# Retention, a dense MoE and a routed MoE on one core: stores, block sums, pass changes and gate sweeps put in another order

## Chip, cores and metric

One core of a Trainium2 chip runs the whole program in one launch. The metric is device microseconds of an execution, taken as the median over runs.

## What is computed

The reference, cut to what matters: a retention (a linear attention with a decaying lower-triangular mask), then a mixture of four experts weighted by given probabilities, then a mixture of eight experts in which each row goes to exactly one expert of limited capacity.

```python
ret = (scale * q @ k.T) * Dmat            # 4 batches, 8 heads, 576 positions, 64 columns a head
x = (ret @ v) as (2304, 512)
p = domain_probs / (domain_probs.sum(-1) + 1e-9)
x = sum_e p[:, e] * (relu(x @ w1[e]) @ w2[e])                     # 4 experts, 512 -> 1024 -> 512
logits = x @ w_gate                                               # 8 experts
rows go to experts greedily by falling logit, at most 288 each
out[row] = relu(x[row] @ moe2_w1[e]) @ moe2_w2[e]
```

All data are 32-bit. The matmuls of both MoE split each operand into a high and a low part (a rounded copy, and the rest) and add three products.

## The kernel before

**Retention** (lines 462 to 623) takes 16 pairs of heads, each as a chain of nine chunks of 64 positions. A chunk is a few 64x64 matmuls (L522, L524), a copy of the state on ScalarE (L533), a masked copy of the scores on VectorE (L535) and the output matmuls (L546); the next chunk of the same pair waits for the copies. Several pairs run interleaved. `finish` multiplies the outputs by the decay (L562 into the tiles `xr` of the first pass, L567 into `xf` tiles) and stores the `xf` tiles to the DRAM tensor `xs` (L573) for the later passes. The order is written by a list scheduler, `Graph`: each operation has an engine, a cost and a bias, and at each step the ready operation of the highest priority goes next. Where the plan leaves TensorE too thinly used, the scheduler sets in small bf16 matmuls (`filler`, L593), a fixed number of them. The same graph carries the preparation of the first MoE: block sums of x (`x_add`, L358, tables `SUMS`), their splits into high and low (`x_split`, L362 and L363, seven tiles x0 to x6; `LOW` names the engine of each low part), and the first two weight blocks `w1_ops(0)` and `w1_ops(1)` (L398 to L400), with their loads (L377) and stores (L384, L385) on the queue of SyncE (SP).

**The first MoE** (lines 626 to 955) makes three passes of 768 rows; a pass has 16 steps `k` (four experts by four blocks of weights), 48 in all. One step uses seven block products (Strassen-like: `step(k, "a")` to `step(k, "g")`, 42 matmuls of 384 columns at L666), each of which needs one x tile and one of the weight parts wa, wt, wb. Between the products stand up to three second-layer tiles of 12 matmuls (`y_next`, L716). Product f of a step goes on in the PSUM bank P, from which `keep(k, 3)` copies on ScalarE (L673) after product e; product g goes on in R, which VectorE reads (`add`, L677) after that copy. So f waits for ScalarE and g for VectorE. The other operations of a step are written by hand between these calls: `some(n)` emits n operations of the weight block of the next step (`early`), `w2_split` splits a second-layer weight (L653, L654), `spare` gives one turn to a side job, `halves` (L448, L449) in the first two passes and `late` in the third. ScalarE, VectorE and GpSimd (POOL) work off their queues in the order written.

At a **pass change** (`turn_`, k = 15 and 31) the seven x tiles are rebuilt from four tiles loaded from `xs`: sums (L358) after product c, then the splits (L362, L363) spread over c to g. All ten (or six) operations of the next weight block come at once after c (`full`); so it is at k = 1 also.

**The third pass's sweeps** (`late`, lines 764 to 810): for the gate logits of the middle rows VectorE makes 48 dot products of a row tile with a gate column (L796), and POOL makes 64 products of a weight tile with a gate column (L802), whose sums ScalarE takes (L791). They come in four sweeps over two gate columns each; in a sweep each turn of `spare` (nine a step) emits one dot product, as long as there are any, and two of three turns a POOL product.

After it the second MoE (from line 959) routes and runs the eight experts; the change doesn't touch its code.

## Time and profile before

| what | value |
|---|---|
| median of 3 runs | 1206.41 us |
| lowest and highest run | 1192.81 and 1209.75 us |
| the profiled execution's own time | 1208.07 us |
| its span, first to last instruction | 1206.3 us |
| mean granted TensorE clock of the span | 0.970 |
| retention, up to the first matmul of the first MoE (L666) | 0 to 127.7 us |
| first pass change, second pass change | near 365 and 626 us |
| third pass, to about | 900 us |

How to read the profile: times are microseconds from the span's start. PE is TensorE, PEld its weight loads, DVE VectorE, ACT ScalarE, SP the queue of SyncE. A row of the stretches gives each engine's busy time in a stretch, then the TensorE clock that was granted (1.00 is 2.4 GHz, 0.50 is 1.2 GHz; a value between is a stretch with both). A row of the timeline gives start, duration, engine, line, operation, and in brackets how long the engine stood idle before it and what ended that.

### The profile page before, as it was taken

Reading aid. Unit: us, or ns where it says so; the run is one execution under the profiler, and the core shown is the slowest. Engines: PE = TensorE matmul, PEld = TensorE weight load, DVE = VectorE, ACT = ScalarE, POOL = GpSimd, SP = SyncE. Lnnn points to the kernel's source line nnn. Section 1 sums busy time; section 2 is a strip of 40 time slices with the busy share of each in tenths; the row PEclk is TensorE's granted clock in tenths of the full one; section 3 lists DMA queues with packets and bytes.
Section 4 is the critical chain, followed back from the end, with each engine's and each line's share of the span. In section 5 each row is a group of like instructions: output and inputs, shape, how many; then the busy total and the mean of one; then the engine's idle time right before and its main releaser. Section 6 shows DMA issues by size and latency. Waiting matters only on the chain. (4 is left out here: it accounts for less than half of the span.)

```text
span 1206.3 us, 22262 instructions
## 1 busy us (share of the span) xinstructions
PE 1165.4 (97%) x8032; PEld 1016.4 (84%) x8032; DVE 716.6 (59%) x1628; ACT 558.0 (46%) x1262; POOL 622.3 (52%) x559
## 2 busy tenths in 40 slices
PE   9999899999999999999999898998999999999997
PEld 7777799999998999998889787887997887888876
DVE  4684466766667354454465767759346766666421
ACT  3442355555555555555453455554640233333332
POOL 5451167777764666766444878879530022222221
PEclk9995799999999999999999899999999999999999
DMA  9673388999984988889644544545311878887780
GB/s 338 199 263 97 113 287 306 331 322 319 334 280 146 314 272 298 300 289 318 224 123 161 195 145 156 198 144 173 99 58 60 322 315 319 319 318 307 301 340 29
DMA packets 125263, 284.43 MB, mean 236 GB/s; under 512 B 14048, under 2 KB 22624, under 8 KB 121056
## 3 DMA queue, kind: packets, MB, share of 16 engines
q1 hardware_dynamic: 121792, 273.23, 64.5%
q0 software_dynamic: 3216, 9.67, 2.2%
q8 instruction: 63, 1.03, 0.4%
q14 instruction: 48, 0.39, 0.1%
q10 hardware_dynamic: 144, 0.11, 0.0%
HBM read 209.00 MB, written 74.19 MB: 235 GB/s over the span
## 5 line engine op out<-in xcount | busy, mean ns | idle before, releaser
L716 PE MATMUL py<-w2h,h 128*128 128x512 f32 x1056 | 350.1, 392 | 0.5 <-ACT h L683 0.5
L716 PEld LDWEIGHTS py<-w2h,h 128*128 128x128 f32 x1056 | 198.3, 188 | 39.0 <-ACT h L683 1.6
L449 POOL TENSOR_TENSOR pair<-pv,pair 128x512 fp32r<-128x512 f32 x128 | 174.8, 1368 | 94.5 <-ACT pair L448 90.5
L716 PE MATMUL py<-w2l,h 128*128 128x512 f32 x528 | 205.5, 389 | 0.0
L673 ACT ACTIVATE sum<-P 128x384 f32<-128x384 f32 x144 | 70.2, 488 | 155.2 <-PE P L666 155.0
L400 POOL TENSOR_TENSOR wal<-r,wah 128x512 fp32r<-128x512 f32 x48 | 64.2, 1337 | 127.1 <-ACT wah L399 94.1
L654 POOL TENSOR_TENSOR w2l<-r,w2h 128x512 fp32r<-128x512 f32 x64 | 89.9, 1406 | 63.1 <-ACT w2h L653 63.0
L723 DVE SCALAR_TENSOR_TENSOR acc<-py,pr,acc 128x512 f32<-128x512 f32 x115 | 85.9, 747 | 56.8 <-PE py L716 56.2
L716 PEld LDWEIGHTS py<-w2l,h 128*128 128x128 f32 x528 | 99.3, 188 | 15.4
L802 POOL TENSOR_TENSOR pp<-pw,wgb 128x512 f32<-128x512 f32 x64 | 98.3, 1551 | 4.2 <-ACT pp L791 2.5
L400 DVE TENSOR_TENSOR wtl<-tw,wth 128x768 fp32r<-128x768 f32 x48 | 61.6, 1284 | 64.2 <-ACT wth L399 64.2
L448 ACT ACTIVATE pair<-pv 128x512 fp32r<-128x512 f32 x128 | 80.2, 627 | 33.9 <-DMA pv<-in_w1b 16.2
L684 DVE SCALAR_TENSOR_TENSOR h<-Q,h 128x384 fp32r<-128x384 f32 x96 | 53.5, 557 | 51.6 <-ACT h L683 51.6
L400 POOL TENSOR_TENSOR wbl<-r,wbh 128x512 fp32r<-128x512 f32 x48 | 77.5, 1615 | 12.7 <-ACT wbh L399 12.7
L229 PE MATMUL ph<-gh,ub 128*128 128x288 f32 x512 | 83.6, 300 | 0.5 <-DVE gl L256 0.3
L683 ACT ACTIVATE h<-Q 128x384 fp32r<-128x384 f32 x96 | 46.8, 487 | 69.8 <-DVE Q L677 69.3
L653 ACT ACTIVATE w2h<-r 128x512 fp32r<-128x512 f32 x96 | 60.3, 628 | 30.5 <-DMA r<-in_w2a 30.4
L229 PEld LDWEIGHTS ph<-gh,ub 128*128 128x128 f32 x512 | 72.3, 188 | 1.5 <-DVE gl L256 1.0
L522 PE MATMUL s<-X,Y 64*64 64x64 f32 x576 | 65.4, 246 | 4.4 <-DVE X L535 3.0
L533 ACT ACTIVATE Y<-s 64x128 f32<-64x128 f32 x128 | 33.7, 269 | 74.5 <-PE s L524 70.5
L1223 POOL DMA_INDIRECT xg<-x_rows,idx x14 | 16.0, 1139 | 99.4 <-DVE idx L256 83.0
L796 DVE SCALAR_TENSOR_TENSOR xt<-row,wgb 128x512 f32<-128x512 f32 x48 | 62.1, 1293 | 8.0 <-DMA row<-x_rows 7.9
(272 smaller groups left out, 2715.2 us busy)
## 6 DMA issues: line engine op xcount, KB each, us to landing
w_halves<-pair SPq DMA_DIRECT2D x64, 512.0 KB, 5.1
ub<-w_halves SPq DMA_DIRECT2D x32, 1024.0 KB, 8.7
r<-in_w2a SPq DMA_DIRECT2D x96, 256.0 KB, 5.2
r<-in_w1a SPq DMA_DIRECT2D x64, 256.0 KB, 4.2
pv<-in_w1b SPq DMA_DIRECT2D x64, 256.0 KB, 4.9
pv<-in_w2b SPq DMA_DIRECT2D x64, 256.0 KB, 5.5
w_low<-pair SPq DMA_DIRECT2D x64, 256.0 KB, 4.3
raw<-in_w2b SPq DMA_DIRECT2D x32, 512.0 KB, 6.6
```

The source lines that it names most:

```text
L229: self.add("pe", cost, lambda: self.nc.tensor.matmul(out, w, x, start=start, stop=stop, **kw), (w, x), (out,), chain=chain, cols=self.size(x))
L400: low = lambda e, i, x: lambda: e.tensor_tensor(w(i, 1), x(), r32(w(i, 0)), op=OP.subtract)
L448: nc.scalar.activation(pair[:, 0], r, AF.Copy)
L449: nc.gpsimd.tensor_tensor(pair[:, 1], r, r32(pair[:, 0]), op=OP.subtract)
L522: nc.tensor.matmul(score()[:, h], Y[lo, h, ch(c + 1)], X[lo, h, ch(c + 1)], start=True, stop=True)
L653: nc.scalar.activation(h, r, AF.Copy)
L654: (nc.vector if i and q < 2 * NPAIR // NP1 else nc.gpsimd).tensor_tensor(lo, r, r32(h), op=OP.subtract)
L673: nc.scalar.activation(sums[n], PS[k]["P"][:, :TG], AF.Copy)
L716: mm(y, x, w, start=(start and n == 0), stop=(stop and n == len(todo) - 1), **kw)
L723: nc.vector.scalar_tensor_tensor(x, y, s, x, op0=OP.mult, op1=OP.add)
L796: nc.vector.scalar_tensor_tensor(scr, row[t], 1.0, wgb[:, e - e0], op0=OP.mult, op1=OP.mult, accum_out=L[:, JT + t, e:e + 1])
L802: nc.gpsimd.tensor_tensor(pp, w[f], wgb[:, e - e0], op=OP.mult)
```

## The change

Two groups of edits. **Retention:** stores of `xf` are held, in the order of the SP queue, behind the load of the pair seven further on (`loads`, `stores`), for which there are four `xf` tiles a kind instead of two; the block sums and splits of x have a bias of 250 instead of 550 and higher planned costs; the first weight block keeps its place, and everything of the second (`w1_load(1)`, `w1_ops(1)`, its store) and the loads behind it come after the last pair's load and with no bias. **First MoE:** at the pass changes the sums have tiles of their own, are emitted after d instead of c, and the splits stand in another order, x1's low part on POOL (`TURN_LOW`); `full` is left to the steps `lone` (0 and 46), so at k = 1, 15 and 31 the next weight block is emitted 3, 3, 2 and 2 at a time, as in other steps; the sweeps run on without a stop between them, with single gate columns loaded ahead (`gate`, four buffers), a dot product at most every second turn and never of a later sweep than the POOL products. Two unused tables of the routing constants go.

```diff
-X_FIRST = 550.0
+X_FIRST = 250.0
...
-            return ("v", 0.86, lambda: nc.vector.tensor_tensor(raw[o], raw[x], raw[y], op=op), (f"r{x}", f"r{y}"), (f"r{o}",))
+            return ("v", 1.4, lambda: nc.vector.tensor_tensor(raw[o], raw[x], raw[y], op=op), (f"r{x}", f"r{y}"), (f"r{o}",))
...
-            en, cost = {"v": (nc.vector, 0.86), "pool": (nc.gpsimd, 1.75)}[e]
+            en, cost = {"v": (nc.vector, 1.2), "pool": (nc.gpsimd, 2.1)}[e]
...
+        TURN_LOW = ("pool", "pool", "pool", "v", "v", "v", "v")
...
-            xfs = [[ld.tile([128, 5 * CK], F32, name=f"xf{k}{i}") for i in range(2)] for k in range(2)]
+            xfs = [[ld.tile([128, 5 * CK], F32, name=f"xf{k}{i}") for i in range(4)] for k in range(2)]
...
+            last = max(loads)
+            for i, op in stores:
+                g.dep(op, loads[min(i + 7, last)], 0.0)
...
-            for q in range(2):
-                g.floor = 50.0 + 12 * q
-                g.add("sp", 0.8, lambda q=q: w1_load(q), (), ("ra", "rb"))
-                for op in w1_ops(q):
-                    g.add(*op)
-                g.add("sp", 1.0, lambda q=q: w1_store(q), ("rb", "tw0", "tw1", "tw2"), ())
-            g.add("sp", 0.8, lambda: w1_load(2), (), ("ra", "rb"))
+            g.floor = 50.0
+            g.add("sp", 0.8, lambda: w1_load(0), (), ("ra", "rb"))
+            for op in w1_ops(0):
+                g.add(*op)
+            g.bias = 0.0
+            late_sp = [g.add("sp", 1.0, lambda: w1_store(0), ("rb", "tw0", "tw1", "tw2"), ())]
+            late_sp.append(g.add("sp", 0.8, lambda: w1_load(1), (), ("ra", "rb")))
+            for op in w1_ops(1):
+                g.add(*op)
...
+            for op in late_sp:
+                g.dep(op, loads[last], 0.0)
...
+                    lag = dots and prods and dots[0][0] > prods[0][0]
+                    if dots and not lag and n % 2:
+                        ahead(dots, row, "row", x_row)
+                        g, t, e = dots.pop(0)
+                        if t == 3:
+                            gate(e + 2)
...
-                full = k == 1 or turn_ or lone
+                full = lone
...
-                if turn_:
-                    wide = lambda x: x.rearrange("p (a n) -> p a n", a=2)
-                    raw[3], raw[4] = wide(hp.tile([128, 768], F32, name="xt")), wide(wl.tile([128, 768], F32, name="tw"))
-                    for x in SUMS[:3]:
-                        x_add(raw, *x)[2]()
-                    split(0)
...
                 if turn_:
-                    split(4, 3)
+                    for i in (3, 4):
+                        raw[i] = room[0].tile([128, 2, TG], F32, name=f"raw{i}")
+                    for x in SUMS[:3]:
+                        x_add(raw, *x)[2]()
+                    split(0)
...
+                if turn_:
+                    split(4)
...
-                    raw[6] = raw[3]
-                    x_add(raw, *SUMS[3])[2]()
-                    split(1, 5)
+                    split(3, 1)
...
+                if turn_:
+                    raw[6] = raw[3]
+                    x_add(raw, *SUMS[3])[2]()
+                    split(5)
```

In the order of the instructions it looks like this. VectorE in retention, before: the two subtractions that begin the second weight block (`tw`, `r`) stand in the middle of the chains of several pairs (X and s are a pair's tiles).

```order
L535 TENSOR_TENSOR X_90<-s_128,tril 64x2x64
L535 TENSOR_TENSOR X_85<-s_129,tril 64x2x64
L398 TENSOR_TENSOR tw<-r_1310,r_1308 128x256
L398 TENSOR_TENSOR r_1310<-r_1310 128x256
L567 TENSOR_TENSOR xf_100<-o_127,gq 128x320
L398 TENSOR_TENSOR tw<-r_1310,tw 128x256
L535 TENSOR_TENSOR X_90<-s_128,tril 64x2x64
L398 TENSOR_TENSOR tw<-r_1308,tw 128x256
```

VectorE in the changed kernel: the same block, up to the last operation of retention and the first one behind it.

```order
L536 TENSOR_TENSOR X_87<-s_128,tril 64x2x64
L397 TENSOR_TENSOR tw<-r_1591,r_1589 128x256
L397 TENSOR_TENSOR r_1591<-r_1591 128x256
L536 TENSOR_TENSOR X_88<-s_130,tril 64x2x64
L397 TENSOR_TENSOR tw<-r_1591,tw 128x256
L536 TENSOR_TENSOR X_87<-s_128,tril 64x2x64
L397 TENSOR_TENSOR tw<-r_1589,tw 128x256
L568 TENSOR_TENSOR xf_99<-o_127,gq 128x256
L536 TENSOR_TENSOR X_88<-s_130,tril 64x2x64
L399 TENSOR_TENSOR wtl<-tw,wth 128x768
L536 TENSOR_TENSOR X_88<-s_130,tril 64x2x64
L568 TENSOR_TENSOR xf_100<-o_131,gq 128x256
```

The block has moved to the last four chunks of retention. On SP, stores of `xf` stood between the loads of later pairs; now each comes behind loads that it stood ahead of, and most stores stand behind the last pair's load.

ScalarE at the first pass change, before (x0h to x6h are the high parts, `sum` is the copy that product f waits for):

```order
L362 ACTIVATE x0h<-raw_4137 128x768
L362 ACTIVATE x4h<-tw 128x768
L362 ACTIVATE x3h<-xt 128x768
L653 ACTIVATE w2h<-r_4150 128x512
L673 ACTIVATE sum_1783<-P 128x384
L362 ACTIVATE x1h<-raw_4139 128x768
```

The same place in the changed kernel:

```order
L360 ACTIVATE x0h<-raw_4128 128x768
L664 ACTIVATE w2h<-r_4141 128x512
L360 ACTIVATE x4h<-raw_4187 128x768
L684 ACTIVATE sum_1774<-P 128x384
L360 ACTIVATE x3h<-raw_4186 128x768
L360 ACTIVATE x1h<-raw_4130 128x768
```

Of the two copies that stood between x4h and `sum`, w2h has gone ahead of x4h and x3h behind `sum`; x4h itself still stands ahead of it. At k = 1 the copy `wth` of the next weight block, which stood two places ahead of w2h and `sum`, now stands behind `sum`.

VectorE at the beginning of the sweeps, before (`xt,L<-row,wgb` is a dot product; `Q<-R,sum` is what product g waits for):

```order
L796 SCALAR_TENSOR_TENSOR xt,L<-row,wgb 128x512
L400 TENSOR_TENSOR wtl<-tw,wth 128x768
L796 SCALAR_TENSOR_TENSOR xt,L<-row,wgb 128x512
L723 SCALAR_TENSOR_TENSOR acc_1767<-py,pr,acc_1767 128x512
L796 SCALAR_TENSOR_TENSOR xt,L<-row,wgb 128x512
L677 TENSOR_TENSOR Q<-R,sum_1783 128x384
L796 SCALAR_TENSOR_TENSOR xt,L<-row,wgb 128x512
```

The changed kernel at the same place:

```order
L821 SCALAR_TENSOR_TENSOR xt,L<-row,wgb 128x512
L399 TENSOR_TENSOR wtl<-tw,wth 128x768
L734 SCALAR_TENSOR_TENSOR acc_1758<-py,pr,acc_1758 128x512
L821 SCALAR_TENSOR_TENSOR xt,L<-row,wgb 128x512
L688 TENSOR_TENSOR Q<-R,sum_1774 128x384
L695 SCALAR_TENSOR_TENSOR h<-Q,h 128x384
L734 SCALAR_TENSOR_TENSOR acc_1759<-py,pr,acc_1759 128x512
L821 SCALAR_TENSOR_TENSOR xt,L<-row,wgb 128x512
```

Of three dot products ahead of `Q<-R,sum` two are left. On POOL a step of the sweeps now always has ten operations: six products, and wal, wbl and two w2l.

## Rows read from the trace of the kernel before

**Rows 1.** The page, part 1: busy time and share of the span of each engine.

```profile
PE 1165.4 (97%) x8032; PEld 1016.4 (84%) x8032; DVE 716.6 (59%) x1628; ACT 558.0 (46%) x1262; POOL 622.3 (52%) x559
```

**Rows 2.** Waits of PE over the span: us in total, times, longest us.

```profile
PE R L666 <- DVE Q L677: 14.1, 8, 3.8
PE P L666 <- ACT sum L673: 10.0, 4, 3.8
```

**Rows 3.** Stretches of retention: PE, PEld, DVE, ACT, POOL busy, PEclk, DMA share, GB/s.

```profile
57.00:93.00 36.00, 31.81 (x566) 25.29 (x568) 32.22 (x68) 15.38 (x45) 22.13 (x16) 0.99 0.78 256
93.00:127.00 34.00, 34.00 (x387) 26.62 (x388) 12.15 (x39) 7.02 (x26) 2.59 (x8) 0.50 0.22 65
```

**Rows 4.** Timeline of VectorE in retention.

```profile
67.50 0.96 DVE L363 TENSOR_TENSOR x5l<-xr,x5h 128x768 fp32r<-128x768 f32 x1
...
87.54 1.31 DVE L398 TENSOR_TENSOR r<-r 128x256 f32<-128x256 f32 x1
```

**Rows 5.** Timeline of step k = 1.

```profile
142.87 0.84 ACT L399 ACTIVATE wth<-tw 128x768 fp32r<-128x768 f32 x1 [2.38 <-DVE tw L398]
...
145.18 1.01 PE L666 MATMUL P<-x2h,wth 128*128 128x384 f32 x2 [3.82 <-ACT sum L673]
```

**Rows 6.** Stretches behind the stalls of k = 1 and of both pass changes.

```profile
144.00:148.00 4.00, 2.82 (x9) 2.83 (x10) 2.61 (x4) 2.62 (x6) 2.76 (x2) 0.50 0.62 204
148.00:152.00 4.00, 4.00 (x18) 4.00 (x17) 1.12 (x2) 0.84 (x3) 0.00 (x0) 0.67 0.55 190
...
368.00:372.00 4.00, 3.95 (x15) 3.63 (x15) 4.00 (x6) 3.91 (x7) 1.79 (x2) 0.64 0.23 57
...
628.00:632.00 4.00, 2.76 (x9) 2.76 (x10) 4.00 (x6) 4.00 (x9) 1.68 (x1) 0.56 0.00 0
632.00:636.00 4.00, 4.00 (x16) 4.00 (x15) 4.00 (x7) 2.13 (x4) 1.97 (x1) 0.58 0.55 166
```

**Rows 7.** Timeline of the first pass change.

```profile
361.78 2.57 POOL L363 TENSOR_TENSOR x0l<-raw,x0h 128x768 fp32r<-128x768 f32 x1
...
362.67 2.49 DVE L358 TENSOR_TENSOR tw<-xt,raw 128x768 f32<-128x768 f32 x1
...
365.19 0.84 ACT L362 ACTIVATE x4h<-tw 128x768 fp32r<-128x768 f32 x1 [4.61 <-DVE tw L358]
...
367.72 0.62 PE L666 MATMUL P<-x2h,wth 128*128 128x384 f32 x2 [2.79 <-ACT sum L673]
```

**Rows 8.** Stretches of the third pass, from 660 us: three of 30 us, one of 5 us, the whole.

```profile
660.00:690.00 30.00, 25.66 (x116) 22.57 (x115) 24.15 (x40) 14.27 (x36) 28.36 (x18) 0.89 0.56 183
720.00:750.00 30.00, 26.78 (x128) 24.14 (x127) 23.41 (x38) 16.37 (x42) 24.95 (x17) 0.94 0.54 176
840.00:870.00 30.00, 29.20 (x147) 27.11 (x148) 12.96 (x22) 17.46 (x52) 17.80 (x16) 0.89 0.39 123
785.00:790.00 5.00, 2.45 (x13) 1.89 (x11) 5.00 (x7) 0.00 (x0) 5.00 (x4) 1.00 0.03 2
660.00:870.00 210.00, 195.40 (x949) 174.32 (x948) 147.51 (x226) 113.14 (x284) 167.76 (x114) 0.96 0.49 160
```

**Rows 9.** Groups of VectorE and POOL, 660 to 870 us, by form; last two 716 to 738.

```profile
L796 DVE SCALAR_TENSOR_TENSOR xt<-row,wgb 128x512 f32<-128x512 f32 x47 | 61.4, 1306 | 4.3 <-DMA row<-x_rows 4.2
L400 DVE TENSOR_TENSOR wtl<-tw,wth 128x768 fp32r<-128x768 f32 x12 | 21.1, 1760 | 8.3 <-ACT wth L399 8.3
L802 POOL TENSOR_TENSOR pp<-pw,wgb 128x512 f32<-128x512 f32 x64 | 98.3, 1551 | 4.2 <-ACT pp L791 2.5 <-DMA row<-x_rows 1.6
...
L802 POOL TENSOR_TENSOR pp<-pw,wgb 128x512 f32<-128x512 f32 x8 | 13.3, 1676 | 0.0
L796 DVE SCALAR_TENSOR_TENSOR xt<-row,wgb 128x512 f32<-128x512 f32 x11 | 14.5, 1319 | 0.0
```

**Rows 10.** Timeline: a dot product and two products of POOL that nothing disturbs.

```profile
672.66 0.80 DVE L796 SCALAR_TENSOR_TENSOR xt<-row,wgb 128x512 f32<-128x512 f32 x1 [1.78 <-DMA row<-x_rows]
...
687.22 2.52 POOL L802 TENSOR_TENSOR pp<-pw,wgb 128x512 f32<-128x512 f32 x2
```

More of the change, by code (lines that the diff above doesn't have):

```diff
@@ L479, in tile_kernel @@
             g.slots = {"ps": [0.0] * NS, "oo": [0.0] * NO}
+            loads, stores = {}, []
             def load(out, src, keys, us):
-                g.add("sp", us, lambda: nc.sync.dma_start(out, src), (), keys, lat=1.05)
+                return g.add("sp", us, lambda: nc.sync.dma_start(out, src), (), keys, lat=1.05)
             lo, hi = slice(0, 64), slice(64, 128)
@@ L497, in pair @@
                     load(X[:, :, cs], a["qk"][b, p, :, :, cs], [k(f"x{c}") for c in range(c0, c1)], 0.182 * (c1 - c0))
-                    load(Y[:, :, cs], a["kv"][b, p, :, :, cs], [k(f"{n}{c}") for n in "kuv" for c in range(c0, c1)],
-                         0.182 * (c1 - c0))
+                    loads[i] = load(Y[:, :, cs], a["kv"][b, p, :, :, cs],
+                                    [k(f"{n}{c}") for n in "kuv" for c in range(c0, c1)], 0.182 * (c1 - c0))
                     if i == 0 and part == 0:
@@ L572, in finish @@
                             if u0 < u1:
-                                g.add("sp", 0.45, lambda u=u, u0=u0, u1=u1: nc.sync.dma_start(
-                                    xs[u - 1, :, p, u0 - u * TP:u1 - u * TP], xf[:, u0 - t0:u1 - t0]), (kx,), (f"xs{i}{c0}{u}",))
+                                stores.append((i, g.add("sp", 0.45, lambda u=u, u0=u0, u1=u1: nc.sync.dma_start(
+                                    xs[u - 1, :, p, u0 - u * TP:u1 - u * TP], xf[:, u0 - t0:u1 - t0]), (kx,), (f"xs{i}{c0}{u}",))))
                     op.give = "oo", cell
@@ L759, in logits @@
                         nc.tensor.transpose(p[:, ks], x[:, ks], ident)
-                    xt = hp.tile([128, 768], F32, name="xt")[:, :D]
+                    xt = hp.tile([128, D], F32, name="xt")
                     nc.scalar.activation(xt, p, AF.Copy)
@@ new lines, in late, with gate @@
+                G0, row, w, todo = {}, {}, {}, []
+                cols = [(e, x) for e in range(0, E2, 2) for x in (0, 1)]
+                dots = [(g, t, g + i) for g in range(0, E2, 2) for t in range(JT) for i in range(2)]
+                prods = [(g, f, g + i) for g in range(0, E2, 2) for f in range(FB) for i in range(2)]
+                def gate(e):
+                    if e < E2 and e not in G0:
+                        G0[e] = q.tile([128, D], F32, name="wgb", bufs=4)
+                        nc.sync.dma_start(G0[e], a["wg"][None, e:e + 1].to_broadcast([128, 1, D]))
@@ new lines, in fetch, with ahead @@
+                def fetch(d, key, name, src, n):
+                    if key not in d:
+                        d[key] = q.tile([128, D], F32, name=name, bufs=2)
+                        nc.sync.dma_start(d[key], src(n))
+                def ahead(todo, d, name, src):
+                    for x in todo[:3]:
+                        fetch(d, x[:2], name, src, x[1])
+                x_row = lambda t: x1d[(JT + t) * 128:(JT + t + 1) * 128]
+                w_row = lambda f: a["w2a"][E1 - 1, f]
+                for e in range(2):
+                    gate(e)
@@ new lines, in late @@
+                fetch(row, dots[0][:2], "row", x_row, 0)
+                fetch(w, prods[0][:2], "pw", w_row, 0)
+                for _ in range(3):
+                    yield
+                n = 0
+                while dots or prods or todo:
+                    n += 1
+                    while todo and (todo[0][0] < n - 2 or not prods):
+                        _, pp, f, e = todo.pop(0)
+                        nc.scalar.activation(pp, pp, AF.Copy, accum_out=M[:, f, e:e + 1])
+                    lag = dots and prods and dots[0][0] > prods[0][0]
[4 more added lines that the diff above has]
+                            gate(e + 2)
+                        scr = hp.tile([128, D], F32, name="xt")
+                        nc.vector.scalar_tensor_tensor(scr, row[g, t], 1.0, G0[e], op0=OP.mult, op1=OP.mult,
+                                                       accum_out=L[:, JT + t, e:e + 1])
+                    if prods and n % 3:
+                        ahead(prods, w, "pw", w_row)
+                        g, f, e = prods.pop(0)
+                        pp = q.tile([128, D], F32, name="pp", bufs=3)
+                        nc.gpsimd.tensor_tensor(pp, w[g, f], G0[e], op=OP.mult)
+                        todo.append((n, pp, f, e))
+                    yield
@@ L856, in split @@
                         x_tile(i)
-                        for op in x_split(raw, i, LOW[i]):
+                        for op in x_split(raw, i, TURN_LOW[i]):
                             op[2]()
```

45 lines of the change are left out of this document (5 added, 40 removed).

## The prediction, made before the changed kernel ran

> **What bounds the kernel now.** I began with the page's busy shares: PE is busy 97% of the span, no other engine over 59% [rows 1]. So the work of the other engines is worth nothing by itself; what can be won is PE's idle time and the time in which PE is busy at half its clock. I therefore read the waits of PE next, then the granted clock by stretches, and last the timelines at each wait.
>
> PE waits little, and in few places: 14.1 us in product g of the first MoE for VectorE's sum, 8 times, and 10.0 us for ScalarE's copy `sum`, 4 times [rows 2]. The clock costs more than that. A stretch at a granted clock c loses about (1 - c) of PE's busy time in it against full speed. In retention the clock is 0.99 up to 93 us, with PE idle for 4.2 of the last 36 us; from 93 to 127 us it is 0.50, half speed, with PE busy 34.00 of 34 us: 34 x 0.5 = 17.0 us lost [rows 3]. The reader should see there that fillers and small matmuls keep PE busy at the lower clock and it stays low until the first MoE's large matmuls begin. The same loss follows the longer stalls later: 2.8 x 0.50 + 4 x 0.33 = 2.7 us at k = 1, by the same sum 1.4 and 2.9 us at the pass changes [rows 6], and some 30 x (0.11 + 0.06 + 0.11) = 8.4 us in the third pass [rows 8]. A stall of 2.79 us at a pass change was followed by the lower clock [rows 6, 7]; a stretch with 2.55 us idle in the third pass was not [rows 8]. [...]
>
> **Retention.** Nothing is added or removed but 13 fillers (293 bf16 matmuls were written, now 280), under 1 us at full speed; work is moved. VectorE is the busy engine before the clock falls, 32.22 of 36 us [rows 3], with the block sums and splits among the chains' masked copies. What fell together with the loss of clock is the second weight block: its subtraction `r` took 1.31 us [rows 4], where the plan counts 0.33, and the chains behind it on VectorE came late where no filler was planned. The change takes that block out of the middle and puts it among the last four chunks, plans 1.2 to 1.4 us for the long VectorE operations, of which an undisturbed one takes 0.96 [rows 4], and lets later pairs' loads go before stores. So I expect the clock to hold until that block, near the end. Then the same 34 us of PE work takes 17, and the price of the block is left: four chunks with a late operation or two and, if the clock falls there, some 6 us at half clock before and after the first matmuls of the MoE, in all about 4 us. Term: 17 - 4 = 13 us gained. Bounds: 19 (all of it, and half of PE's 4.2 us of idle time before) to 0 (it falls at the same place), and below nothing in rival 3. The stores moved on SP cost nothing as long as four `xf` tiles suffice: a store's tile is wanted again by the pair four further on, and the load it waits behind needs only the pair one further on to have ended. The first reader of `xs` comes at the first pass change.
>
> **k = 1.** ScalarE stood 2.38 us in `wth`, waiting for VectorE's `tw`, with w2h and `sum` behind it, and PE waited 3.82 us for `sum` [rows 5]. With `wth` behind `sum`, what is ahead of it are wah and w2h, both free to run; about 0.6 us of PE's wait stays, 3.2 go. The clock's 2.7 us [rows 6] go too. Late next is VectorE's `Q<-R,sum` behind the four subtractions, and the second-layer tile of step 2; I set 0.9 us against that. Term: 5.0 us; 2 to 6.
>
> **Pass changes.** ScalarE's x4h waited 4.61 us for the second sum on VectorE, which took 2.49 us beside POOL's x0l of 2.57; `sum` stood behind x4h, x3h and w2h, and PE waited 2.79 us [rows 7]. The order of the changed kernel keeps x4h ahead of `sum`, and VectorE's wtl and three sums come in the same order as before, so x4h starts as late. Only x3h and w2h go from the way: x4h takes 0.84 us [rows 7], x3h is as large, w2h two thirds of it, 0.84 + 0.56 = 1.4 us. So 1.4 us of wait stay at each change, short enough for the clock. Gain: 2 x 1.4 + 1.4 + 2.9 = 7.1 us. x1l, moved to POOL, runs there at about 2.57 us behind x0l and w2l and is needed by product b of the next step, nearly at once; I take 0.5 us off. Term: 6.6 us; 2 if the clock falls all the same, 10 if no stall is left.
>
> **Sweeps.** 48 dot products stay, at 1.31 us plus a read of the accumulator [rows 9], but in every second turn of nine instead of each: 4.5 a step instead of 9. From 660 to 870 us there are 12 steps (12 wtl [rows 9]), so a step took 17.5 us; without the 14.1 us of stalls and 8.4 us of clock it is (210 - 22.5)/12 = 15.6. VectorE without dot products is busy (147.5 - 61.4)/12 = 7.2 us a step [rows 8, 9]. With nine it needs 7.2 + 9 x 1.31 = 19.0, more than a step: it falls behind until the sweep's dot products end, and product g waits, up to 3.8 us [rows 2]. With 4.5 it needs 7.2 + 5.9 = 13.1 of 15.6: it keeps up. I leave 3.5 us for short stalls. Term: 14.1 + 8.4 - 3.5 = 19.0 us; 6 to 22. What covers it is POOL, which now gets six products in every step, with no pause between sweeps. POOL's other work is (167.8 - 98.3)/12 = 5.8 us a step [rows 8, 9]; with six products of 1.55 us it needs 15.1 of 15.6 us. That is 97%: it just keeps up.
>
> **Sum.** 13 + 5.0 + 6.6 + 19 = 43.6 us off the profiled execution's 1208.07: 1164 us. That execution lies 1.7 us above the median of the runs shown, which is less than their spread of 16.9; I make no correction.
>
> **A rule that speaks against it.** The trace shows that VectorE and POOL slow each other: a product takes 1.68 us where dot products are dense, 1.55 in the mean [rows 9]. The Trainium skill, "SBUF — State Buffer", section "Who interferes with whom", says that a VectorE instruction with two SBUF inputs and a GpSimd instruction that reads SBUF take a shared port in turn, the second blocked until the first ends. By that rule no two of them overlap. The trace agrees only in part: undisturbed, a dot product took 0.80 us and a product 1.26 [rows 10], so each does hold the other up; but the 11 dot products and 8 products of 716 to 738 us would fill 8.8 + 10.1 = 18.9 us in turn, and POOL's other work, 22 - 13.3 = 8.7 us of that stretch [rows 9], some 8.7 x 1.26/1.68 = 6.5 more: 25.4 in 22 us. They do overlap.
>
> **Rivals.**
> 1. *The clock falls in retention where it fell before*, since other long VectorE operations (the splits, now spread further) open the same gaps. For it: VectorE's 32.22 of 36 us is work that stays. Against it: gaps up to 92 us didn't lower the clock. Price: the 13 us. Time 1177.
> 2. *POOL becomes the bound of the sweeps.* At the dense price of 1.68 in place of 1.55, POOL needs 15.1 x 1.68/1.55 = 16.4 us a step, over the 10.7 steps of the 64 products (0.8 us a step) 9 us more than PE's 15.6; w1 and w2 low parts come late and PE waits. Against it: dot products are half as dense. Time 1173; with rival 1, 1186. By the rule in full the operations would run in turn, at the undisturbed times: ten of POOL at 1.26 us, 4.5 dot products at 0.80 [rows 10] and wtl at 0.96 [rows 4] make 17.2 us a step, 17 us more than PE's over the 10.7 steps, and 1181.
> 3. *Slower than before.* The clock falls early in retention, as the first block sums crowd VectorE. From 57 us on, the 31.8 us of PE work to 93 us [rows 3] would take twice as long, on top of what was lost before: 1164 + 13 + 31.8 = 1209. So a fall at 56 us or before decides; each microsecond earlier adds one, and at 50 us it is 1216. Against it: the block sums now come later and with more time planned.
> 4. *The moves do nothing where PE waits*: the stalls at the pass changes and in the sweeps come back as long, behind other operations (x4h still ahead of `sum`). Then retention and k = 1 alone count: 1208 - 18 = 1190.
>
> **How the numbers follow.** Forecast 0.45, its own range 1153 to 1175. Rival 1 alone 0.18, rival 2 alone 0.13 (the rule in full 0.02 of it), both together 0.08, rival 3 0.05, rival 4 0.07; better than the forecast's range 0.04. Two per cent of 1206.41 is 24 us, about what a measurement can tell from no change: faster means under 1182. That holds for the forecast, rivals 1 and 2 apart and the better case: 0.78 with what their spread costs. Rivals 4 and both together are within 2%, with most of 3: 0.17. Slower 0.05. The range goes from 1148 to 1190.
>
> **What would show it.** Right: clock 1.00 from 60 us to shortly before the first L666, which starts near 112 to 116 us; PE's wait at k = 1 under 1 us; at the pass changes one wait of 1.2 to 1.7 us for `sum`, clock 1.00 after it; no wait of product g over 1.5 us in the third pass, POOL busy over 95% there, and pp at 1.5 to 1.6 us. Wrong: the first L666 after 125 us (rival 1 or 3); waits of PE for wal, wbl or w2l, or of ScalarE for a load behind a stuck product load (rival 2); `Q<-R,sum` still behind three dot products.

## The result, and the profile after

The changed kernel takes 1170.88 us (median of 4 executions, 1168.69 to 1175.64), the kernel before 1205.09 (4 executions, 1192.81 to 1209.75): ratio 0.973, 95% interval 0.966 to 0.980. It is faster, by 34 us in the medians; the forecast was 1164, 42.4 us less than the median then known. Over all the sessions below the kernel before took 1189 to 1199 us at a mean granted clock of 0.982 to 0.991, or 1201 to 1215 us at 0.963 to 0.980; its profiled execution (0.970) is one of the longer ones, and as the ratios leave some of the longest out, they need not be the ratio of two medians. The profiled execution of the changed kernel took 1171.26 us, 36.8 less than that of before.

Where these 36.8 us came from is read best from marks that both traces have: the first matmul of product c of a step, at L666 before and at L677 now. "c15 to c17" is the time from product c of step 15 to that of step 17.

| stage | before, us | after, us | gained | forecast |
|---|---|---|---|---|
| retention, up to c0 | 129.94 | 111.76 | 18.2 | 13 |
| k = 1, c0 to c2 | 24.73 | 20.59 | 4.1 | 5.0 |
| first pass change, c15 to c17 | 39.13 | 42.88 | -3.8 | 3.3 |
| second pass change, c31 to c33 | 36.82 | 40.65 | -3.8 | 3.3 |
| sweeps, c33 to c47 | 238.71 | 215.00 | 23.7 | 19 |
| the steps between these | 423.90 | 423.56 | 0.3 | 0 |
| second MoE, c47 to the end | 313.07 | 315.06 | -2.0 | 0 |

In this pair of traces two terms came out larger than forecast, and the pass changes have the wrong sign. The page's busy row of the changed kernel answers to [rows 1]:

```profile
PE 1141.1 (98%) x8019; PEld 997.2 (85%) x8019; DVE 710.7 (61%) x1626; ACT 559.9 (48%) x1262; POOL 622.8 (53%) x561
```

PE is busy 24 us less with nearly the same matmuls, as more of them run at the full clock, and idle 12 us less. Its waits over the span answer to [rows 2]:

```profile
PE py L727 <- ACT h L694: 5.4, 3, 3.1
PE P L677 <- ACT sum L684: 4.3, 4, 1.5
PE R L677 <- DVE Q L688: 4.0, 3, 1.4
```

Product g waits 3 times instead of 8, and f, for `sum`, 4.3 instead of 10.0 us. New is the row on top: second-layer tiles (`py`) wait for ScalarE's `h`; before, that was 0.5 us in all.

Retention by stretches, in the columns of [rows 3]:

```profile
57.00:93.00 36.00, 34.36 (x702) 28.48 (x700) 31.68 (x81) 16.31 (x56) 15.05 (x11) 1.00 0.64 208
93.00:100.00 7.00, 7.00 (x128) 5.50 (x124) 3.61 (x11) 2.68 (x10) 0.00 (x0) 1.00 0.93 301
100.00:104.00 4.00, 2.49 (x43) 1.94 (x40) 3.68 (x6) 1.31 (x4) 2.87 (x3) 1.00 0.23 87
104.00:108.00 4.00, 3.53 (x39) 2.84 (x38) 2.18 (x5) 1.11 (x2) 1.45 (x7) 0.53 0.76 165
108.00:112.00 4.00, 4.00 (x18) 3.88 (x19) 1.30 (x6) 0.49 (x1) 0.00 (x0) 0.62 0.95 311
```

PE executes 702 matmuls from 57 to 93 us where it executed 566, and the clock stays at 1.00 up to 104 us. There, at the second weight block, it falls for some 7 us, over the stage's end: the first matmul at L677 comes at 108.31 us, 19.4 earlier than before. The fall belongs to this execution: in the traces of e1, e4, e7 and e8 below, whose retention is the same, the clock does not fall there, and c0 comes at 109.0 to 110.0 us.

The third pass answers to [rows 8] and [rows 9] (two stretches, then two groups of 660 to 810 us):

```profile
660.00:690.00 30.00, 30.00 (x153) 27.26 (x152) 23.93 (x41) 19.81 (x50) 29.07 (x21) 1.00 0.62 201
720.00:750.00 30.00, 30.00 (x154) 27.30 (x153) 23.24 (x40) 18.78 (x48) 29.13 (x20) 1.00 0.57 180
...
L821 DVE SCALAR_TENSOR_TENSOR xt<-row,wgb 128x512 f32<-128x512 f32 x43 | 45.8, 1065 | 0.0
...
L827 POOL TENSOR_TENSOR pp<-pw,wgb 128x512 f32<-128x512 f32 x58 | 89.1, 1557 | 0.3 <-DMA pw<-in_w2a 0.2
```

PE has no gap and full clock; POOL is busy 29.07 and 29.13 of 30 us, 97%, its products at 1.56 us as before, and yet PE doesn't wait for it. The dot products fell from 1.31 to 1.07 us.

The first pass change is where the loss is. Its timeline, all engines, rows that the argument needs:

```profile
337.24 2.01 POOL L399 TENSOR_TENSOR wbl<-r,wbh 128x512 fp32r<-128x512 f32 x1
338.01 6.51 DVE L356 TENSOR_TENSOR raw<-raw,raw 128x768 f32<-128x768 f32 x3
339.21 2.56 POOL L361 TENSOR_TENSOR x0l<-raw,x0h 128x768 fp32r<-128x768 f32 x1
342.61 0.84 ACT L360 ACTIVATE x4h<-raw 128x768 fp32r<-128x768 f32 x1 [3.20 <-DVE raw L356]
343.89 0.62 PE L677 MATMUL P<-x2h,wth 128*128 128x384 f32 x2 [1.54 <-ACT sum L684]
345.38 2.35 POOL L361 TENSOR_TENSOR x1l<-raw,x1h 128x768 fp32r<-128x768 f32 x1 [1.67 <-ACT x1h L360]
345.98 0.55 DVE L688 TENSOR_TENSOR Q<-R,sum 128x384 f32<-128x384 f32 x1
346.45 2.10 DVE L361 TENSOR_TENSOR x3l<-raw,x3h 128x768 fp32r<-128x768 f32 x1
346.58 1.01 PE L677 MATMUL R<-x6h,wbh 128*128 128x384 f32 x2 [1.36 <-DVE Q L688]
349.50 1.84 POOL L361 TENSOR_TENSOR x2l<-raw,x2h 128x768 fp32r<-128x768 f32 x1 [1.76 <-ACT x2h L360]
349.60 2.28 DVE L665 TENSOR_TENSOR w2l<-r,w2h 128x512 fp32r<-128x512 f32 x1
351.80 0.95 DVE L356 TENSOR_TENSOR raw<-raw,raw 128x768 f32<-128x768 f32 x1
352.84 0.85 ACT L360 ACTIVATE x6h<-raw 128x768 fp32r<-128x768 f32 x1 [3.42 <-DVE raw L356]
355.13 0.50 PE L727 MATMUL py<-w2h,h 128*128 128x512 f32 x1 [1.52 <-ACT h L694]
```

Product f waits 1.54 us, as forecast. But g waits 1.36 us, too, for `Q<-R,sum`, which comes on VectorE behind the three block sums (6.51 us), `acc` and x4l, and in step 16 a second-layer tile waits for ScalarE's `h`: x6h stands 3.42 us for VectorE's fourth sum, with the next step's copies `sum` and `h` queued behind it. In the kernel before, the fourth sum came directly behind `Q<-R,sum`, and x6h did not wait:

```profile
368.47 0.56 DVE L677 TENSOR_TENSOR Q<-R,sum 128x384 f32<-128x384 f32 x1
368.94 0.95 DVE L358 TENSOR_TENSOR xt<-raw,tw 128x768 f32<-128x768 f32 x1
...
371.07 0.84 ACT L362 ACTIVATE x6h<-xt 128x768 fp32r<-128x768 f32 x1
```

At the second change of the changed kernel the same three waits take 1.54, 1.38 and 3.09 us. The stretches of the first change lose clock:

```profile
344.00:348.00 4.00, 2.64 (x10) 2.31 (x11) 4.00 (x5) 2.74 (x5) 2.35 (x1) 0.82 0.00 0
348.00:352.00 4.00, 4.00 (x18) 3.91 (x18) 4.00 (x5) 1.42 (x3) 1.84 (x1) 0.75 0.00 0
...
356.00:360.00 4.00, 4.00 (x15) 3.86 (x16) 1.77 (x4) 2.47 (x5) 0.89 (x1) 0.60 0.50 168
```

### The profile page after: what moved, and what is told of

It is laid out like the page before. It is cut to its first block, busy times and chain, and to the rows that moved or that the text cites. A ratio compares the mean times of both kernels' runs of the same rounds, so it can differ in the third digit from the quotient of the medians.

```text
span 1169.5 us, 22235 instructions
## 1 busy us (share of the span) xinstructions
PE 1141.1 (98%) x8019; PEld 997.2 (85%) x8019; DVE 710.7 (61%) x1626; ACT 559.9 (48%) x1262; POOL 622.8 (53%) x561
## 5 line engine op out<-in xcount | busy, mean ns | idle before, releaser
L665 POOL TENSOR_TENSOR w2l<-r,w2h 128x512 fp32r<-128x512 f32 x64 | 87.4, 1366 | 34.2 <-ACT w2h L664 34.2
L399 POOL TENSOR_TENSOR wbl<-r,wbh 128x512 fp32r<-128x512 f32 x48 | 79.4, 1654 | 13.7 <-ACT wbh L398 10.1
L507 POOL TENSOR_TENSOR Y<-Y,gk 64x576 f32<-64x576 f32 (+2 forms) x36 | 38.1, 1079 | 42.1 <-DMA Y<-in_kv 31.2
L523 PE MATMUL s<-X,Y 64*64 64x64 f32 x576 | 55.7, 228 | 2.1 <-DVE X L536 1.9
```

The source lines that it names most:

```text
L399: low = lambda e, i, x: lambda: e.tensor_tensor(w(i, 1), x(), r32(w(i, 0)), op=OP.subtract)
L523: nc.tensor.matmul(score()[:, h], Y[lo, h, ch(c + 1)], X[lo, h, ch(c + 1)], start=True, stop=True)
L665: (nc.vector if i and q < 2 * NPAIR // NP1 else nc.gpsimd).tensor_tensor(lo, r, r32(h), op=OP.subtract)
```

## Experiments on the pass changes

Each kernel below was timed against the kernel before on the same chip; that one had medians of 1199 to 1206 us in the four sessions. After each time stands the ratio to it, with its 95% interval. The changed kernel itself was not timed again in these sessions. A difference to it in us is therefore one between medians of different sessions, and the stages of the traces are set beside it.

**e1: the order of before.** In the changed kernel only the order of the pass changes was set back:

```diff
-                        for op in x_split(raw, i, TURN_LOW[i]):
+                        for op in x_split(raw, i, LOW[i]):
...
-                full = lone
+                full = turn_ or lone
```

with sums and `split(0)` after c, `split(4, 3)` after d, the fourth sum and `split(1, 5)` after e.

> The changed kernel with the pass changes alone set back to the order of the kernel before: the whole next weight block at once behind product c, the three sums behind it, then x0, then x4 and x3 behind d, the fourth sum, x1 and x5 behind e, x2, x6; x1's low part on VectorE; the sums keep tiles of their own. Theory: the new order itself is what costs; from product c of step 15 to that of step 17 it took 42.9 us against 39.1 before, and from c of step 31 to that of step 34 56.1 against 53.6, so undoing it gives back 6 us: 1165 us, with one wait of PE of 2.5 to 3 us for the copy sum at each change and none of a y tile for ScalarE's h. Rival: the new waits come from something else that changed (loads that land later, POOL's jobs); then it stays at 1171 and the wait of a y tile for h stays.

Measured: 1161.25 us (ratio 0.967, 0.959 to 0.975). c15 to c17 took 39.05 us, c31 to c33 35.89: 8.6 us less than in the changed kernel. PE waits 2.79 us for `sum` once at each change, and the tile's wait for `h` at the changes is gone. The wait at the first change:

```profile
344.48 0.62 PE L677 MATMUL P<-x2h,wth 128*128 128x384 f32 x2 [2.79 <-ACT sum L684]
```

How much the new order costs is read from all traces that have one order or the other. In the five with the new one (the changed kernel and e4, e5, e9 and e10 below) the two changes take 79.4 to 83.5 us together, in the four with the old one (the kernel before, e1, e3 and e6) 74.9 to 76.0. So the new order costs 3.5 to 8.7 us, 6.5 in the mean, and the trace of the changed kernel is the longest of its five. The old order, with one long wait, was better than the new one with two or three.

**e2: low parts on VectorE.** `TURN_LOW = ("v", "v", "v", "v", "v", "v", "v")`.

> The changed kernel with the low parts of x0, x1 and x2 at the pass changes on VectorE instead of POOL. Theory: an operation of VectorE with two inputs in SBUF does not run while POOL has one there (x3l took 2.10 us beside POOL's x1l and ended 0.8 us behind it, alone 0.94; the three sums took 6.5 us beside wbl and x0l); POOL's 1.8 us each then cost VectorE more than its own 0.94. The three sums end near 342, 1.6 us earlier, f waits some 0.5 us, g hardly, x6h waits no longer and the y tile of step 16 does not wait for h: 1160 to 1164 us. Rival: VectorE simply has too much to do there, and three more operations of 0.94 us make the fourth sum and x6h 1 to 3 us later: 1174 to 1178 us, with a longer wait of the y tile.

Measured: 1166.53 us (0.970, 0.962 to 0.978). The changes took 39.57 and 38.01 us, 6.0 less in all than in the changed kernel and 1.9 less than in the best of the five traces with its order, though VectorE has three more operations at each. Its waits at the first change:

```profile
348.37 0.62 PE L677 MATMUL P<-x2h,wth 128*128 128x384 f32 x2 [1.08 <-ACT sum L684]
350.86 0.61 PE L677 MATMUL R<-x6h,wbh 128*128 128x384 f32 x2 [1.17 <-DVE Q L688]
358.38 0.50 PE L727 MATMUL py<-w2h,h 128*128 128x512 f32 x1 [2.08 <-ACT h L694]
```

Both theories hold in part: POOL's operations held VectorE up (f and g wait less, at both changes), and VectorE is overfull as well (the tile waits 2.08 us here instead of 1.52). At the second change the tile waits 2.05 us instead of 3.09, so the second half is not clear. The median is 4.4 us under the changed kernel's, less than forecast, and the two ratios' intervals overlap.

**e7: `sum` ahead of x4h.** From e1, `split(4, 3)` was moved from behind d to behind e.

> The changed kernel with the pass changes in the order of before (1161 us so far), but with x4 and x3 split behind product e, so that ScalarE's copy sum stands ahead of x4h and x3h and no longer behind their wait for VectorE's second sum. Theory: the wait of 2.79 us for sum at each change, and the lower clock behind it (0.74 and 0.83, then 0.67 and 0.91, of 4 us each), come from x4h ahead of sum; both go, 4 to 5 us a change: 1152 to 1154 us. Rival: VectorE, full from 336 to 352 us, is the bound there; the wait comes back as one of product g or of a y tile for h: 1158 to 1162 us.

Measured: 1166.72 us (0.975, 0.966 to 0.983), 5 us slower than e1; the changes took 41.18 and 38.05 us, 4.3 more. The rival was right on the place, and its time was 4 us too short:

```profile
344.56 0.62 PE L677 MATMUL R<-x6h,wbh 128*128 128x384 f32 x2 [2.35 <-DVE Q L688]
349.79 0.62 PE L677 MATMUL Q<-x1l,wah 128*128 128x384 f32 x2 [0.59 <-DVE x1l L361]
353.85 0.50 PE L727 MATMUL py<-w2h,h 128*128 128x512 f32 x1 [1.37 <-ACT h L694]
```

f waits no more, and its wait turns up at g, at product b of the next step and at the tile. What VectorE has to do, together with the time that it stands still for POOL, bounds the stretch; the place of one copy on ScalarE only chooses which product waits.

**e8: splits spread into the next step.** x0 and x1 are split behind c; the low parts of x4 and x3, the fourth sum, x5, x2 and x6 come in steps 16 and 32, and x1's low part is on VectorE. The low part of step 15's and 31's second `w2` goes to POOL, and the side jobs pause until the moved work is done.

```diff
+                if after_turn:
+                    low(4, 3)
+                    raw[6] = raw[3]
+                    x_add(raw, *SUMS[3])[2]()
```

> The changed kernel with a new order of the pass changes: the blocks of x0 and x1 loaded first and split at once behind product c (low parts on VectorE), the three sums behind d, x4h and x3h behind the copy sum, their low parts, the fourth sum, x5, x2 and x6 in the next step, where nothing is late yet; the low part of the second w2 of step 15 on POOL. Theory: at each change VectorE and POOL have more to do before the next step's first y tile than fits, because what both do in SBUF runs in turn; with five low parts and one sum moved behind that tile no wait over 1 us is left, step 15 to 16 takes 15.5 to 17 us instead of 22.7: 1148 to 1154 us. Rival: the moved work lands on the next step's own weights (wtl, wbl) and on the halves' jobs and makes product a or d of step 17 wait: 1156 to 1163 us.

Measured: 1167.68 us (0.976, 0.968 to 0.985), over both forecasts. The second change took 35.30 us, the first 43.28: there step 16 to 17 took 23.12 us, as the moved work met the logit transposes that follow the first pass alone; they waited 2.0 us for VectorE's `acc`. And g waited 2.84 us for `Q<-R,sum` at both changes, where the theory left no wait over 1 us. So the rival, with other victims than it named.

**e11: the sums one step earlier.** Blocks loaded and all four sums done in steps 14 and 30:

```diff
+                if blocks_:
+                    for i in (3, 4, 6):
+                        raw[i] = room[0].tile([128, 2, TG], F32, name=f"raw{i}")
+                    for x in SUMS[:2]:
+                        x_add(raw, *x)[2]()
...
-                spare(False)
+                spare(u == 1)
```

> The changed kernel with the blocks of a pass change loaded one step earlier (steps 14 and 30) and all four sums done there, where VectorE has time; in step 15 and 31 the splits alone, x0 and x1 behind product c, x4 behind d, x3 and x5 about f, x2 and x6 behind f and g; x1's low part on VectorE. The halves' jobs end a step earlier (58 pieces in the first pass, one turn more a step in the second). Theory: the copies of ScalarE stood behind sums of VectorE, and VectorE behind POOL; with the sums done before, neither is left: steps 15 to 16 and 31 to 32 take 16 to 18 us instead of 22.7 and 23.0 (20.5 and 20.4 in the order of before), 1150 to 1156 us. Rival: seven low parts and the locks of POOL alone already fill VectorE: a wait of 2 us and the lower clock stay: 1158 to 1163 us.

Measured: 1193.54 us (0.998, 0.994 to 1.003), a miss in the time and right in the place: the changes took 37.51 and 34.37 us, the best so far, but the steps between them 34 us more than in the changed kernel. The extra turn of `spare` in every step of the second pass ran the halves' copies ahead of their loads:

```profile
451.97 0.63 ACT L447 ACTIVATE pair<-pv 128x512 fp32r<-128x512 f32 x1 [4.53 <-DMA pv<-in_w2b]
452.51 0.47 ACT L684 ACTIVATE sum<-P 128x384 f32<-128x384 f32 x1
...
453.03 1.01 PE L677 MATMUL P<-x5h,wbh 128*128 128x384 f32 x2 [4.97 <-ACT sum L684]
```

**e12: the same, with three extra turns of the halves** (in steps 16 to 18, instead of one in every step of the second pass), and later splits: x4 behind `Q<-R,sum`, x3 and x2 behind f, x5 and x6 in the next step behind `h<-R`:

```diff
-                spare(u == 1)
+                spare(16 <= k < 19)
...
+                if u and kk == 0:
+                    split(5, 6)
```

> As the kernel with the sums one step earlier, with its loss mended: the second pass's halves get three turns more (steps 16 to 18) instead of one in every step, where ScalarE's copies waited up to 4.5 us for their loads with the copy sum behind them (25.3 us of waits of PE, 11 times). At the changes x4 is split behind e, x3 and x2 behind f, x5 and x6 in the next step behind h<-R, so that no low part stands ahead of Q<-R,sum or of h. Theory: the pass changes took 37.5 and 34.4 us there (product c of step 15 to 17, of 31 to 33) against 42.9 and 40.7 in the changed kernel, and 39.1 and 35.9 in the order of before; with the last two waits of 1.2 us gone they take some 35 and 32, 16 us less than in the changed kernel: 1153 to 1158 us against 1171, and 3 to 8 us under the order of before (1161). Rival: loads of halves are at their limit in the second pass with any of its work squeezed into two steps less; waits for the copy sum stay in steps 20 to 28: 1162 to 1175 us.

Measured: 1156.98 us (1153.65 to 1159.90, 6 executions; ratio 0.965, 0.960 to 0.970). The changes took 36.06 and 31.16 us, 16.3 less than in the changed kernel, and the trace lists no wait of PE in steps 15, 31 and 32. The median is 14 us under the changed kernel's, and no execution of the one lies in the range of the other. The 4 us under e1 are not shown by the times, as the ratios (0.965 and 0.967) lie within each other's intervals; but the two changes take 67.2 us here, where the four traces of the old order have 74.9 to 76.0. What is left at the first change is one wait of 1.53 us for `acc` in step 16. The steps between the changes took 3.1 us more than in the changed kernel, with waits for `sum` again.

## Experiments on the other parts

**e3: retention alone** (the kernel before with the first group of edits; the two unused tables go here, too).

> The kernel before with the retention part of the change alone. Theory: the 18.2 us by which the first step's product c came earlier in the changed kernel are retention's own, and nothing behind it depends on them: 1205 - 18 = 1187 us, first matmul of the first MoE near 108 us. Rival: the gain needs the MoE part or is used up behind (waits that move, the same end of the stage): above 1195 us.

Measured: 1187.91 us (10 executions; 0.990, 0.986 to 0.995), c0 at 109.81 us. The part stands alone. By the ratio it is worth some 12 us (6 to 17), not the 18.2 of the table: those are the gain over one execution of before, whose clock stood at 0.50 for 34 us of retention [rows 3], and other executions of it were 15 us shorter, at a higher mean clock.

**e4: sweeps of before** (`late` as in the kernel before, all else changed).

> The changed kernel with the sweeps of the third pass alone as in the kernel before: four sweeps apart, double gate tiles, a dot product in every turn. Theory: they are worth the 22.4 us that lie between product c of step 34 and that of step 47 in the two traces: 1171 + 22 = 1193 us, with waits of product g for VectorE of up to 3.8 us again. Rival: part of the gain came from the loads or from POOL standing differently behind the earlier stages: 1178 to 1186 us.

Measured: 1188.73 us (0.989, 0.981 to 0.997), 17.9 slower than the changed kernel. c33 to c47 took 239.70 instead of 215.00 us, so the sweeps are worth 24.7 between these two traces; the rest of the difference (c0 2.3 us earlier here, and less lost behind the pass changes) lies outside them. All four traces with the old sweeps (the kernel before, e3, e4, e6) have 236.0 to 239.7 us there, all others 215.0 to 216.8. Product g waits 17.5 us again, 10 times.

**e5 and e6: the second weight block.** e5 puts it back to 62 us in the changed kernel, e6 moves it alone in the kernel before:

```diff
+            for q in range(2):
+                g.floor = 50.0 + 12 * q
+                g.add("sp", 0.8, lambda q=q: w1_load(q), (), ("ra", "rb"))
```

> The changed kernel with the second weight block of retention back where it was (its load from 62 us on, the priority of the first block), all else of the retention part as changed. Theory: that block in the middle of the chains is what lowers the clock; it falls near 87 to 100 us again and the first matmul of the first MoE comes at 118 to 127 us instead of 108: 1181 to 1189 us. Rival: the lower priority and higher planned costs of the block sums, or the stores that wait, keep the clock: within 3 us of 1171.

> The kernel before with one edit of the retention part alone: the second weight block, its store and the loads behind it come after the last pair's load and with no priority. Theory: it is worth most of the retention part, whose 18.2 us were measured alone: 1187 to 1193 us against 1206. Rival: it needs the other retention edits (priority 250, planned costs, stores held), without which the block sums lower the clock: 1200 to 1207 us.

Measured: e5 1170.69 us (0.980, 0.971 to 0.989), the changed kernel's time, c0 at 110.58. e6 1194.35 (0.997, 0.993 to 1.002), c0 at 120.65, between its two forecasts; by its interval no difference from before is shown. In e5 the block runs in the middle of the chains, from 84 us, and the clock stays at 1.00:

```profile
84.00:88.00 4.00, 3.94 (x80) 3.20 (x77) 3.72 (x11) 2.18 (x6) 1.05 (x1) 1.00 0.98 350
88.00:92.00 4.00, 4.00 (x70) 3.29 (x66) 3.84 (x7) 0.59 (x3) 3.84 (x4) 1.00 0.51 166
```

My theory for retention falls with this: where the block stands decides nothing, as long as the other edits are in. Its `r` took 0.41 us there, against the 1.31 of [rows 4], where POOL's `wal` ran beside it.

**e9 and e10: the other two edits undone**, each alone in the changed kernel: the stores no longer held; priority and planned costs as before.

```diff
-                g.dep(op, loads[min(i + 7, last)], 0.0)
+                pass
```

```diff
-X_FIRST = 250.0
+X_FIRST = 550.0
```

> The changed kernel with the stores of retention no longer held behind later loads (four xf tiles kept). The block's place alone is not what keeps the clock (block back early: 1170.7 us; block late alone: 1194.4 us, first product c at 120.7 us against 109 to 112), so one of the other retention edits does. Theory: the priority of 250 and the planned costs of the block sums do it, the held stores next to nothing (PE waited 1.2 us for a late Y before): first product c near 110 to 113 us and 1169 to 1174 us. Rival: the held stores do it: first product c at 117 to 121 us and 1177 to 1182 us.

> The changed kernel with the priority (550) and the planned costs (0.86, 0.86 and 1.75 us) of the block sums and splits as before; stores held, second weight block late. Theory: these edits carry what the block's late place alone did not, some 8 to 10 us: first product c at 117 to 121 us and 1178 to 1183 us. Rival: the held stores carry it: first product c near 110 us and 1169 to 1174 us.

Measured: e9 1173.49 us (1170.61 to 1186.34; 0.986, 0.970 to 1.002), c0 at 114.94 with the clock at 1.00, between its two forecasts: at most a few us, not told apart from nothing. e10 1181.88 us (1178.49 to 1186.60; 0.989, 0.976 to 1.001), 11 slower than the changed kernel, no execution of the one within the range of the other. In its profiled execution, the longest of the four, c0 comes at 131.08:

```profile
56.00:60.00 4.00, 2.53 (x42) 1.92 (x41) 3.91 (x8) 1.96 (x3) 3.92 (x2) 1.00 0.03 6
60.00:64.00 4.00, 3.67 (x63) 2.90 (x59) 3.87 (x7) 1.94 (x6) 1.86 (x2) 0.71 0.74 228
64.00:84.00 20.00, 20.00 (x211) 15.60 (x209) 14.86 (x28) 5.99 (x17) 10.10 (x8) 0.50 0.56 189
...
112.00:124.00 12.00, 12.00 (x122) 9.26 (x121) 3.54 (x11) 1.62 (x6) 0.00 (x0) 0.50 0.41 138
```

With the block sums at high priority VectorE and POOL are full (3.91 and 3.92 of 4 us), PE idles 1.5 us, and the clock falls near 62 us already, comes back near 86 and falls again near 109. So the lower priority and the larger planned costs of the block sums carry most of the retention part, 11 of some 12 us by the times. Which of the two does it was not tried; and that full engines are what brings the clock down is read from this one trace, not shown by an edit of its own.

## Why the prediction was right, and where it was wrong

- **Faster, within the range.** 1170.88 lies in 1148 to 1190 and in the forecast's own 1153 to 1175. The sum was 43.6 us, measured between the two profiled executions were 36.8: 5.2 too little for retention, 4.7 too little for the sweeps, 0.9 too much for k = 1, 14.2 too much for the pass changes, 2.0 for the second MoE not foreseen. That the total lies so near owes something to luck: errors of both signs cancel. Three of the four terms had the right size to within 6 us, and the fourth had the wrong sign.
- **The step that failed: the pass changes, "So 1.4 us of wait stay at each change, short enough for the clock".** The wait itself came at 1.54 us, twice. What the step left out is all that queues on VectorE behind it. I counted what stands ahead of `sum` on ScalarE and took 0.5 us off for x1l; but VectorE's fourth sum now comes behind x3l, h, acc and w2l, and x3l and w2l stood still while POOL worked, 2.10 and 2.28 us for operations of 0.94 and 0.68. The result was three waits at each change instead of one, and lower clock: -7.6 us instead of +6.6 in this trace. Against it e1 gives back 8.6, e2 6.0, e12 16.3; as the five traces of this order differ by 4.1 us, some 2 of each are this trace's own. "Short enough for the clock" failed as well: the clock fell behind waits of 1.54 and 1.36 us. At k = 1 waits of the same size (0.56, 0.64 and 1.05 to 1.26 us) left the clock at 1.00 in seven traces and were followed by a lower one in e1, e7, e8 and e11, so no run shows a length of stall that is safe. Rival 4 had the place and the mechanism, one operation behind another, for this half; I gave it 0.07.
- **Retention: size right in the mean, cause wrong.** The term was 13 with bounds of 0 and 19; measured were 18.2 between the two traces, and some 12 over executions (e3). "What fell together with the loss of clock is the second weight block" was true of the trace of before and was no cause: e5 has the block early and keeps the clock, e10 has it late and loses it. The end went as written in the one trace, a block that costs some us near 104; in e1, e4, e7 and e8, with the block at the same place, the clock did not fall there. Block sums that crowd VectorE, the mechanism of rival 3, are what stands ahead of the first fall in e10; what brought the clock down at 93 us in the kernel before was not isolated.
- **k = 1:** waits of 0.56, 0.64 and 1.23 us, clock 1.00; 4.1 of 5.0 us. The wait for `sum` came as counted (0.6); in e1, e7, e8 and e11, where the clock fell at these waits, c0 to c2 took 22.0 to 22.2 us instead of 20.59, so the term is 2.6 there.
- **Sweeps: right, size too small.** POOL at 97% (forecast 97), pp at 1.56 us (1.55), no wait of g there. "I leave 3.5 us for short stalls" was not needed, and 23.7 lies over the upper bound of 22. Rival 2 did not come: PE waited nowhere in the sweeps for an operation of POOL.
- **Second MoE.** PE's wait for a gather was 2.2 us instead of 2.0, and here the clock fell behind it (0.65 from 1122 to 1126 us), where before it stayed at 1.00. The change doesn't touch that code, and over all traces the stage takes 312.2 to 315.1 us; the 2 us are no part of it.

## What to carry to other kernels

Where two operations change places, redo the queues of every engine that takes part up to the next point at which all of them are idle, not only the one whose wait is to go: a shorter wait on ScalarE was paid with two on VectorE. If the stretch is bound by one engine (VectorE at 4.00 of 4 us for 8 us on end, the time that it stood still for POOL included), another order within it only moves the wait (e7); move work out of the stretch, to where that engine has time (e12), and not into a step that is full itself (e8 at the first change). And an operation that stands beside a stall in one trace is a suspect, not a cause, until it has been moved by itself (e5).

## What the runs showed that I had not expected

VectorE's operations with both inputs in SBUF, and POOL's, took turns. I had written "They do overlap". In e12 the chain shows it without a break (start, duration):

```profile
336.95 1.85 POOL L361 TENSOR_TENSOR x0l<-raw,x0h 128x768 fp32r<-128x768 f32 x1 [0.17 <-ACT x0h L360]
337.64 1.98 DVE L361 TENSOR_TENSOR x1l<-raw,x1h 128x768 fp32r<-128x768 f32 x1 [1.89 <-ACT x1h L360]
338.76 2.01 POOL L399 TENSOR_TENSOR wbl<-r,wbh 128x512 fp32r<-128x512 f32 x1
339.54 2.05 DVE L399 TENSOR_TENSOR wtl<-tw,wth 128x768 fp32r<-128x768 f32 x1
340.73 2.01 POOL L665 TENSOR_TENSOR w2l<-r,w2h 128x512 fp32r<-128x512 f32 x1
```

x1l ends 0.82 us after x0l, wbl 1.15 after x1l, wtl 0.82 after wbl, w2l 1.15 after wtl: in each step nearly the whole time that the operation takes alone (0.95 and 1.29). The time that an operation stands shows in the profile as its duration, not as a wait. In the changed kernel's timeline above, x3l ends 0.82 us after x1l, w2l 0.54 after x2l. An operation with an input in PSUM isn't held: `Q<-R,sum` took 0.55 us there, in the middle of x1l. This is the rule of the Trainium skill, "SBUF — State Buffer", section "Who interferes with whom", that such operations exclude each other; the trace agrees.

My count against it took for each operation of the sweeps its time alone (for a dot product 0.80 us; one at 721.20 us took 0.67), where in turn it adds less. The stretch that I counted, in the kernel before, shows it:

```profile
729.82 1.75 POOL L802 TENSOR_TENSOR pp<-pw,wgb 128x512 f32<-128x512 f32 x1
730.46 1.67 DVE L796 SCALAR_TENSOR_TENSOR xt<-row,wgb 128x512 f32<-128x512 f32 x1
731.53 1.75 POOL L400 TENSOR_TENSOR wbl<-r,wbh 128x512 fp32r<-128x512 f32 x1
732.05 2.04 DVE L400 TENSOR_TENSOR wtl<-tw,wth 128x768 fp32r<-128x768 f32 x1
733.24 1.99 POOL L654 TENSOR_TENSOR w2l<-r,w2h 128x512 fp32r<-128x512 f32 x1
734.01 1.76 DVE L796 SCALAR_TENSOR_TENSOR xt<-row,wgb 128x512 f32<-128x512 f32 x1
```

A dot product ends some 0.55 us after the operation of POOL ahead of it, wtl 0.81, and an operation of POOL some 1.15 after that of VectorE. The 11 dot products, 13 operations of POOL and one wtl of 716 to 738 us make 11 x 0.55 + 13 x 1.15 + 0.81 = 21.8 us in turn, in a stretch of 22: "They do overlap" was wrong, and no overlap is left to show. At these sizes rival 2's ten operations of POOL, 4.5 dot products and one wtl of a step make 14.8 us in turn instead of its 17.2, which fits in the 15.4 that a step of the changed sweeps took (215.00/14). So the rule in full, priced like this, lets VectorE and POOL keep up, as they did.

The clock in retention differs from execution to execution of the same code. In [rows 3] it stayed at 0.50 for 34 us with PE busy throughout; in the profiled execution of e10 it came back after some 24 us (rows above), in that of e6 after 7. In e2, whose retention is the changed kernel's, it fell near 75 us and came back after 17, with c0 at 116.72. So in these traces the change makes the fall rarer or shorter, and does not exclude it. That the spread of the kernel before, 1189 to 1215 us, goes with the granted clock is shown by the mean clocks given with the result; that it is the clock of retention is likely, and was not shown, as one execution of it was profiled.
